# A retention block with a max-out feed-forward on one core: queries and keys of 28 chunks transposed by VectorE in 32x32 blocks instead of by TensorE

## The chip, the core and the metric

The kernel runs on one core of a Trainium2 chip. A core has five engines that run side by side and wait for each other through semaphores: TensorE (PE in the profile; its weight loads are shown apart as PEld), VectorE (DVE), ScalarE (ACT), GpSimd (POOL) and SyncE (SP), which here only issues DMAs. The metric is the device time of one execution in microseconds (us). Unchanged, the kernel takes 888.28 us (median of three runs, 887.31 to 889.44).

## The reference

Inputs are `q`, `k`, `v` of 8 batches x 8 heads x 576 positions x 64, float32, and four weight matrices in float64. Two parts follow each other:

```
# retention, per batch and head; gamma depends on the head
scores = (q @ k.T) / sqrt(64)
ret    = scores * (gamma ** (i - j) where i >= j, else 0)
x      = ret @ v                      # to [8 * 576, 8 * 64] = [4608, 512]
# feed-forward, w1, w2, w3: [512, 768], w_out: [768, 512]
h   = max(x @ w1, x @ w2, x @ w3)
out = h @ w_out                       # [4608, 512]
```

## The kernel before, in words

**Chunks.** The 8 x 576 = 4608 positions are cut into 36 chunks of 128 (`C`), `g` = 0 to 35. A chunk holds all 8 heads as 4 pairs (`NP`); a pair fills 128 partitions, 64 per head. For a chunk the kernel does, in this order:

- `load(g)`: one DMA each for k, q and v (two where a chunk crosses a batch), issued on SP; positions go on partitions, so a row of 8 heads x 64 numbers lands per partition.
- `decay_keys(g)`: GpSimd multiplies the keys by `gk`, gamma to the power minus the position (line 130).
- `transposes(g)`: TensorE transposes the decayed keys and the queries, four 128x128 pieces each, into PSUM (line 141); VectorE copies the keys (line 144), ScalarE the queries (line 146) to SBUF, as `kT` and `qT`.
- `scores(g)`: 8 matmuls of `kT` and `qT` (line 155), two masking products on VectorE (line 158), then 4 matmuls `kv` of keys and values (line 166) that bring the running state forward (lines 169 to 172).
- `values(g)`: 8 matmuls of the masked scores with v, and 4 of the old state with `qT` (lines 185, 190); VectorE multiplies by `gq`, gamma to the power plus the position, and the scale (line 192), into `xT`, the transposed input of the feed-forward.

**Groups.** Four chunks make a block of 512 tokens, `t` = 0 to 8, for the feed-forward `ffn(t)`. Block 0 multiplies plainly (`up_plain`), while the float64 weights are converted to float32 by VectorE, ScalarE and GpSimd (`conversion`). From block 1 on, `up` does each of 9 units (3 pairs of feature blocks x 3 weights) as seven half-size products (line 292), whose results VectorE and ScalarE combine: line 297 copies, lines 310, 320 and 323 add, lines 325, 331 and 332 take maxima. A unit needs line 320 to be done before its seventh product writes the same PSUM tile. Four `down` products (line 338) with a ScalarE copy and a DMA out on SP (lines 341, 342) end a block.

**Order.** The order is written out by hand. While block `t` runs, the chunks of block `t+1` are put between its units: `transposes`, one unit, `scores`, one unit, `values`, one unit, then the next chunk. So the block's first three chunks stand between the nine units, and the fourth chunk's steps before the first, second and third `down`. `load(g+1)` is called just before `transposes(g)`, and `decay_keys(g+1)` just before `scores(g)`. Each engine takes its own instructions strictly in this order; SP too, so a load that stands behind the DMAs out of a block is issued after them. DMAs on SP take eight semaphores in turn: each waits until the eighth DMA before it has landed. Raw tiles have four buffers each for k, q and v; a load also waits until its buffer has been read.

Of the kernel before, what the change touches and what calls it, by code (L numbers as in the profile page):

```python
# [26 lines left out]
FP32 = mybir.dt.float32  # L30
# [7 lines left out]
C = 128  # L38
NT = 4 * C
NH = NT // 2  # L40
AHEAD = 3
WAHEAD = 3

# [2 lines left out]
def kernel(  # L46
# [23 lines left out]
    CPT = NT // C  # L70
# [3 lines left out]
    wraw = ctx.enter_context(tc.tile_pool(name="wraw", bufs=WAHEAD))  # L74
    wtmp = ctx.enter_context(tc.tile_pool(name="wtmp", bufs=2))
    raw = ctx.enter_context(tc.tile_pool(name="raw", bufs=AHEAD + 1))
    kpool = ctx.enter_context(tc.tile_pool(name="kpool", bufs=3))
    att = ctx.enter_context(tc.tile_pool(name="att", bufs=2))
    stp = ctx.enter_context(tc.tile_pool(name="stp", bufs=2))
    xpool = ctx.enter_context(tc.tile_pool(name="xpool", bufs=2))  # L80
# [9 lines left out]
    gk = const.tile([C, H], FP32, name="gk")  # L90
# [14 lines left out]
    def start_of(g):  # L105
        r = -g * C % S
        return r if r < C else None

    masks = {0: causal, None: causal}
    for r in sorted({start_of(g) for g in range(NG)} - {0, None}):  # L110
        m = masks[r] = const.tile([C, C], FP32, name=f"causal{r}")
# [1 line left out]
        nc.gpsimd.memset(m[0:r, r:C], 0.0)  # L113


    raws, kds, qks, sts, states = {}, {}, {}, {}, {}

    def load(g):
        for n, src in (("k", k), ("q", q), ("v", v)):
            t = raws[n, g] = raw.tile([C, H, D], FP32, tag=n, name=n + "raw")  # L120
            row = 0
            while row < C:
                b, pos = divmod(g * C + row, S)
                n = min(C - row, S - pos)
                nc.sync.dma_start(t[row:row + n], src[b, :, pos:pos + n, :].rearrange("h p d -> p h d"))
                row += n

    def decay_keys(g):
        t = kds[g] = kpool.tile([C, H, D], FP32, tag="kd", name="kd")
        nc.gpsimd.tensor_tensor(t[:], raws.pop(("k", g))[:], gk[:].unsqueeze(2).to_broadcast([C, H, D]),  # L130
                                op=ALU.mult)

    def pair(t, p):
        return t[:, 2 * p:2 * p + 2, :].rearrange("a h d -> a (h d)")

    def transposes(g):
        both = {}
        for n, src in (("k", kds[g]), ("q", raws.pop(("q", g)))):
            pt = ps_r.tile([P, NP, C], FP32, tag="r", name=n + "t")
            for p in range(NP):  # L140
                nc.tensor.transpose(pt[:, p, :], pair(src, p), ident[:C, :C])  # L141
            t = both[n] = att.tile([P, NP, C], FP32, tag=n + "T", name=n + "T", bufs=2 if n == "k" else 3)
            if n == "k":
                nc.vector.tensor_copy(t[:], pt[:])
            else:
                nc.scalar.copy(t[:], pt[:])
        qks[g] = both

    def scores(g):
        qT, kT = qks[g]["q"], qks[g]["k"]  # L150
        s = [ps_r.tile([C, NP, C], FP32, tag="r", name=f"s{j}") for j in range(2)]
        for p in range(NP):
            for j in range(2):
                r = slice(D * j, D * (j + 1))
                nc.tensor.matmul(s[j][:, p, :], lhsT=kT[r, p, :], rhs=qT[r, p, :], start=True, stop=True)  # L155
        st = sts[g] = att.tile([C, 2, NP, C], FP32, tag="st", name="st", bufs=2)
        for j in range(2):
            nc.vector.tensor_tensor(st[:, j], s[j][:], masks[start_of(g)][:].unsqueeze(1).to_broadcast([C, NP, C]),  # L158
                                    op=ALU.mult)
        kd = kds.pop(g)  # L160
        if g + 1 == NG or start_of(g + 1) == 0:
            return
        r = start_of(g) or 0
        kv = ps_r.tile([P, NP, P], FP32, tag="r", name="kv")
        for p in range(NP):
            nc.tensor.matmul(kv[:, p, :], lhsT=pair(kd, p)[r:], rhs=pair(raws["v", g], p)[r:], start=True, stop=True)  # L166
        t = states[g + 1] = stp.tile([P, NP, P], FP32, tag="state", name="state")
        if start_of(g) is not None:
            nc.vector.tensor_tensor(t[:], kv[:], gs[:], op=ALU.mult)
        else:  # L170
            nc.vector.tensor_tensor(t[:], kv[:], states[g][:], op=ALU.add)  # L171
            nc.gpsimd.tensor_tensor(t[:], t[:], gs[:], op=ALU.mult)  # L172
# [3 lines left out]
    def values(g):  # L176
        old = C if start_of(g) is None else start_of(g)
        t, i = divmod(g, CPT)
        if i == 0:
            xT[t] = xpool.tile([P, NDC, NT], FP32, tag="xT", name="xT")  # L180
        st, vr, qT = sts.pop(g), raws.pop(("v", g)), qks.pop(g)["q"]
        o = ps_r.tile([P, NP, C], FP32, tag="r", name="o")
        for p in range(NP):
            for j in range(2):
                nc.tensor.matmul(o[D * j:D * (j + 1), p, :], lhsT=vr[:, 2 * p + j, :], rhs=st[:, j, p, :],  # L185
                                 start=(p == 0), stop=(old == 0 and p == NP - 1), skip_group_check=True)
        if old > 0:
            sd = states.pop(g)
            for p in range(NP):
                nc.tensor.matmul(o[:, p, :old], lhsT=sd[:, p, :], rhs=qT[:, p, :old],  # L190
                                 start=False, stop=(p == NP - 1), skip_group_check=True)
        nc.vector.tensor_tensor(xT[t][:, :, i * C:(i + 1) * C], o[:], gq[:], op=ALU.mult)  # L192
        if i == CPT - 1 and t > 0:
            x = xT[t]
            a11, a12, a21, a22 = (x[:, 2 * d:2 * d + 2, NH * r:NH * (r + 1)] for r in range(2) for d in range(2))
            s1, s2, s3, s4 = (spool.tile([P, 2, NH], FP32, tag=f"S{n}", name=f"S{n}") for n in (1, 2, 3, 4))
            nc.vector.tensor_tensor(s1[:], a21, a22, op=ALU.add)
            nc.vector.tensor_tensor(s2[:], s1[:], a11, op=ALU.subtract)
            nc.gpsimd.tensor_tensor(s3[:], a11, a21, op=ALU.subtract)
            nc.gpsimd.tensor_tensor(s4[:], a12, s2[:], op=ALU.subtract)  # L200
            xS[t] = {1: a11, 2: a12, 3: s4[:], 4: a22, 5: s1[:], 6: s2[:], 7: s3[:]}
# [77 lines left out]
    def convert(n):  # L279
        for _ in range(n):  # L280
            next(converting, None)

    def up(t, h, fp, i):

        f0, f1, lo, hi = 2 * fp, 2 * fp + 1, slice(0, NH), slice(NH, NT)
        x = ps_x.tile([P, NH], FP32, tag="x", name="x")
        y = {}
# [7 lines left out]
        def kept(name, src):  # L295
            c = ppool.tile([P, NH], FP32, tag=name, name=name)
            nc.scalar.copy(c[:], src[:])  # L297
            return c
# [77 lines left out]


    load(0)
    load(1)
    load(2)  # L380
    load_weights(1)
    load(3)
    load_weights(2)
    decay_keys(0)
    decay_keys(1)
    transposes(0)
    transposes(1)
    decay_keys(2)
    scores(0)
    transposes(2)  # L390
    values(0)
    decay_keys(3)
# [9 lines left out]
    decay_keys(4)  # L402
    convert(2)
    values(3)
    convert(4)
    for t in range(N // NT):
        work = ffn(t)
        for g in range((t + 1) * CPT, (t + 2) * CPT):
            for step in (transposes, scores, values):
                if g < NG:  # L410
                    if step is transposes and g + 1 < NG:
                        load(g + 1)
                    if step is scores and g + 1 < NG:
                        decay_keys(g + 1)
                    step(g)
                next(work, None)

# [50 lines left out]
```

## Time and profile before

| | |
|---|---|
| median of three runs | 888.28 us (887.31 to 889.44) |
| profiled execution, its own time | 889.22 us |
| its span, first to last instruction | 887.5 us |
| PE busy | 870.8 us, 98% of the span |
| DVE, ACT, POOL busy | 371.4, 185.8, 141.4 us |
| mean granted clock of TensorE | 0.996 |
| moved by the DMA queue of SP | 50.34 MB in 128064 packets |

Busy shares are means over stages with different limits, so the stretches of the span are looked at apart: a start of some 35 us in which the first chunks are loaded and computed, the block with the weight conversion up to about 145 us, seven blocks of 93 to 96 us each with four chunks in them, and a last block without chunks. An idle time in the profile carries the name of what ended it; idle time of an engine that nobody waits for costs nothing. Matmul durations overlap, so that the time a group of matmuls takes is read from the start of its first to the start of what follows.

### The profile page before, as it was taken

Reading aid. Unit: us, or ns where it says so; the run is one execution under the profiler, and the core shown is the slowest. Engines: PE = TensorE matmul, PEld = TensorE weight load, DVE = VectorE, ACT = ScalarE, POOL = GpSimd, SP = SyncE. Lnnn points to the kernel's source line nnn. Section 1 sums busy time; section 2 is a strip of 40 time slices with the busy share of each in tenths; the row PEclk is TensorE's granted clock in tenths of the full one; section 3 lists DMA queues with packets and bytes.
Section 4 is the critical chain, followed back from the end, with each engine's and each line's share of the span. In section 5 each row is a group of like instructions: output and inputs, shape, how many; then the busy total and the mean of one; then the engine's idle time right before and its main releaser. Section 6 shows DMA issues by size and latency. Waiting matters only on the chain.

```text
span 887.5 us, 11310 instructions
## 1 busy us (share of the span) xinstructions
PE 870.8 (98%) x4544; PEld 639.5 (72%) x4544; DVE 371.4 (42%) x681; ACT 185.8 (21%) x391; POOL 141.4 (16%) x128
## 2 busy tenths in 40 slices
PE   6999989999999999999999999999999999999998
PEld 5645546887588858885788668875888578866883
DVE  3899944553244423443244324432433334422330
ACT  2455521111111102111111111111111111111211
POOL 3444424221110111001210011101111111001000
PEclk9999989999999999999999999999999999999999
DMA  9545614200150006000600033001600050000001
GB/s 235 154 138 173 179 49 121 57 1 12 57 123 1 1 36 154 1 1 24 147 21 1 13 96 83 1 1 49 142 1 1 24 130 1 0 25 24 1 1 47
DMA packets 128547, 51.58 MB, mean 58 GB/s; under 512 B 113648, under 2 KB 122864, under 8 KB 128496
## 3 DMA queue, kind: packets, MB, share of 16 engines
q1 hardware_dynamic: 128064, 50.34, 21.5%
q8 instruction: 36, 0.59, 0.3%
q10 hardware_dynamic: 432, 0.53, 0.2%
q14 instruction: 15, 0.12, 0.0%
HBM read 41.42 MB, written 9.44 MB: 57 GB/s over the span
## 4 chain that ended last, share of the span: by engine, by line
PE 87%; DVE 5%; ACT 3%; issue 2%; POOL 1%; DMA 1%; SPq 0%; DVEq 0%; POOLq 0%; ACTq 0%
PE x L292 28%; PE down L338 21%; PE z L292 14%; PE y L292 7%; PE s L155 4%; PE o L185 3%; PE kv L166 3%; PE o L190 3%; PE kt L141 2%; PE qt L141 2%; ACT expo L244 1%; ACT expo L248 1%; DVE expo L241 1%; DVE expo L252 1%; DVE h L352 1%
## 5 line engine op out<-in xcount | busy, mean ns | idle before, releaser
L338 PE MATMUL down<-wout,h 128*128 128x512 f32 x432 | 191.7, 597 | 3.8 <-POOL wout L255 3.8
L338 PEld LDWEIGHTS down<-wout,h 128*128 128x128 f32 x432 | 80.5, 191 | 96.5 <-issue 90.7
L292 PE MATMUL x<-S,T 128*128 128x256 f32 x576 | 147.8, 379 | 0.0
L292 PEld LDWEIGHTS x<-S,T 128*128 128x128 f32 x576 | 109.2, 190 | 15.1
L172 POOL TENSOR_TENSOR state<-state,gs 128x512 f32<-128x512 f32 x24 | 31.5, 1311 | 343.5 <-DVE state L171 296.5
L158 DVE TENSOR_TENSOR st<-s,causal 128x512 f32<-128x512 f32 x72 | 46.4, 686 | 76.5 <-PE s L155 76.5
L292 PE MATMUL x<-xT,w 128*128 128x256 f32 x288 | 74.9, 382 | 0.0
L292 PE MATMUL x<-S,w 128*128 128x256 f32 x288 | 74.3, 380 | 0.0
L292 PE MATMUL z<-xT,T 128*128 128x256 f32 x288 | 73.9, 379 | 0.0
L292 PE MATMUL z<-S,w 128*128 128x256 f32 x288 | 73.9, 379 | 0.0
L292 PE MATMUL y<-xT,w 128*128 128x256 f32 x288 | 73.9, 379 | 0.0
L297 ACT COPY p<-x 128x256 f32<-128x256 f32 x72 | 26.8, 372 | 182.8 <-PE x L292 182.8
L320 DVE TENSOR_TENSOR tmp<-x,p 128x256 f32<-128x256 f32 x48 | 20.4, 425 | 104.4 <-PE x L292 104.4
L347 PE MATMUL up<-xT,w 128*128 128x512 f32 x144 | 63.4, 593 | 0.0
L341 ACT COPY osb<-down 128x512 f32<-128x512 f32 x36 | 21.1, 586 | 202.1 <-PE down L338 202.1
L292 PEld LDWEIGHTS z<-S,w 128*128 128x128 f32 x288 | 54.7, 190 | 7.4
L292 PEld LDWEIGHTS y<-xT,w 128*128 128x128 f32 x288 | 54.7, 190 | 7.4
L292 PEld LDWEIGHTS z<-xT,T 128*128 128x128 f32 x288 | 54.1, 189 | 8.1
L292 PEld LDWEIGHTS x<-S,w 128*128 128x128 f32 x288 | 49.4, 189 | 13.2 <-issue 1.1
L192 DVE TENSOR_TENSOR xT<-o,gq 128x512 f32<-128x512 f32 x36 | 24.8, 690 | 72.8 <-PE o L190 66.8
L292 PEld LDWEIGHTS x<-xT,w 128*128 128x128 f32 x288 | 49.8, 191 | 5.5 <-issue 0.8
L130 POOL TENSOR_TENSOR kd<-kraw,gk 128x512 f32<-128x512 f32 x36 | 38.3, 1068 | 85.5 <-DMA kraw<-in_k_dram 74.9
(61 smaller groups left out, 913.9 us busy)
## 6 DMA issues: line engine op xcount, KB each, us to landing
bits<-in_moe_w_dram SPq DMA_DIRECT2D x18, 512.0 KB, 3.6
out_dram<-osb SPq DMA_DIRECT2D x36, 256.0 KB, 2.0
kraw<-in_k_dram SPq DMA_DIRECT2D x32, 256.0 KB, 4.0
qraw<-in_q_dram SPq DMA_DIRECT2D x32, 256.0 KB, 4.3
vraw<-in_v_dram SPq DMA_DIRECT2D x32, 256.0 KB, 4.3
bits<-in_moe_w_out_dram SPq DMA_DIRECT2D x6, 512.0 KB, 3.4
kraw<-in_k_dram SPq DMA_DIRECT2D x8, 128.0 KB, 3.6
qraw<-in_q_dram SPq DMA_DIRECT2D x8, 128.0 KB, 3.2
```

The lines of the kernel that those rows point to most:

```text
L130: nc.gpsimd.tensor_tensor(t[:], raws.pop(("k", g))[:], gk[:].unsqueeze(2).to_broadcast([C, H, D]), op=ALU.mult)
L141: nc.tensor.transpose(pt[:, p, :], pair(src, p), ident[:C, :C])
L155: nc.tensor.matmul(s[j][:, p, :], lhsT=kT[r, p, :], rhs=qT[r, p, :], start=True, stop=True)
L158: nc.vector.tensor_tensor(st[:, j], s[j][:], masks[start_of(g)][:].unsqueeze(1).to_broadcast([C, NP, C]), op=ALU.mult)
L166: nc.tensor.matmul(kv[:, p, :], lhsT=pair(kd, p)[r:], rhs=pair(raws["v", g], p)[r:], start=True, stop=True)
L172: nc.gpsimd.tensor_tensor(t[:], t[:], gs[:], op=ALU.mult)
L185: nc.tensor.matmul(o[D * j:D * (j + 1), p, :], lhsT=vr[:, 2 * p + j, :], rhs=st[:, j, p, :], start=(p == 0), stop=(old == 0 and p == NP - ...
L190: nc.tensor.matmul(o[:, p, :old], lhsT=sd[:, p, :], rhs=qT[:, p, :old], start=False, stop=(p == NP - 1), skip_group_check=True)
L292: nc.tensor.matmul(out[:], lhsT=w[:, d * P:(d + 1) * P], rhs=xS[t][n][:, d, :], start=first and d == 0, stop=d == 1, skip_group_check=True)
L297: nc.scalar.copy(c[:], src[:])
L338: nc.tensor.matmul(ps[:], lhsT=h[:, fb, m * P:(m + 1) * P], rhs=w_sb["out", fb][:], start=(fb == 0), stop=(fb == NF - 1))
L347: nc.tensor.matmul(ps[:], lhsT=w_sb[i, fb][:, dc * P:(dc + 1) * P], rhs=xT[t][:, dc, :], start=(dc == 0), stop=(dc == NDC - 1))
```

## The change

Chunks 0 to 7 are transposed by TensorE as before (`BY_PE = 8`). For chunks 8 to 35:

- Queries are loaded in 32x32 blocks: 16 DMAs of 32 partitions x 4 pairs x 32 numbers (128 bytes in one piece, 16 KB each) per chunk. The keys are loaded so as well, in another 16 DMAs, into a tile `kx`. A block lands where it has to stand after its own transposition.
- VectorE transposes every 32x32 block in place of its row, one instruction of 128x512 for the keys and one for the queries, from SBUF to SBUF. There are no transposes on TensorE and no copies from PSUM for these chunks.
- The keys are also loaded as rows, as before, for the `kv` matmuls.

For all chunks the decay is taken off the keys and put on the values: GpSimd multiplies v by the same `gk` (`decay_values`), so the transposes read raw keys, and `kv` and the score-value products read decayed values. Buffers: q 4, `kx` 2, v 3, k rows 4. In chunks 4 to 7 the copy of the transposed keys moves from VectorE to ScalarE.

```
+BY_PE = 8
-    kpool = ctx.enter_context(tc.tile_pool(name="kpool", bufs=3))
+    vpool = ctx.enter_context(tc.tile_pool(name="vpool", bufs=3))
...
+    def spans(g):
+        row = 0
+        while row < C:
+            b, pos = divmod(g * C + row, S)
+            n = min(C - row, S - pos)
+            yield row, b, pos, n
+            row += n
 
     def load(g):
-        for n, src in (("k", k), ("q", q), ("v", v)):
-            t = raws[n, g] = raw.tile([C, H, D], FP32, tag=n, name=n + "raw")
...
+        rows = (("k", k), ("q", q), ("v", v)) if g < BY_PE else (("k", k), ("v", v))
+        for n, src in () if g < BY_PE else (("q", q), ("kx", k)):
+            t = raws[n, g] = raw.tile([P, NP, C // 32, 32], FP32, tag=n, name=n + "raw", bufs=4 if n == "q" else 2)
+            for blk in range(C // 32):
+                b, pos = divmod(g * C + 32 * blk, S)
+                for a in range(4):
+                    nc.sync.dma_start(
+                        t[32 * a:32 * a + 32, :, blk, :],
+                        src[b, a // 2::2, pos:pos + 32, 32 * (a % 2):32 * (a % 2) + 32].rearrange("p j i -> j p i"))
+        for n, src in rows:
+            t = raws[n, g] = raw.tile([C, H, D], FP32, tag=n, name=n + "raw", bufs=3 if n == "v" else 4)
+            for row, b, pos, m in spans(g):
+                nc.sync.dma_start(t[row:row + m], src[b, :, pos:pos + m, :].rearrange("h p d -> p h d"))
 
-    def decay_keys(g):
-        t = kds[g] = kpool.tile([C, H, D], FP32, tag="kd", name="kd")
-        nc.gpsimd.tensor_tensor(t[:], raws.pop(("k", g))[:], gk[:].unsqueeze(2).to_broadcast([C, H, D]),
+    def decay_values(g):
+        t = vds[g] = vpool.tile([C, H, D], FP32, tag="vd", name="vd")
+        nc.gpsimd.tensor_tensor(t[:], raws.pop(("v", g))[:], gk[:].unsqueeze(2).to_broadcast([C, H, D]),
                                 op=ALU.mult)
...
     def transposes(g):
-        both = {}
-        for n, src in (("k", kds[g]), ("q", raws.pop(("q", g)))):
+        both = qks[g] = {}
+        if g >= BY_PE:
+            for n in ("k", "q"):
+                t = both[n] = att.tile([P, NP, C], FP32, tag=n + "T", name=n + "T", bufs=2 if n == "k" else 3)
+                nc.vector.transpose(t[:].rearrange("a p c -> a (p c)"),
+                                    raws.pop(("kx" if n == "k" else n, g))[:].rearrange("a p b i -> a (p b i)"))
+            return
+        for n, src in (("k", raws["k", g]), ("q", raws.pop(("q", g)))):
...
-            if n == "k":
+            if n == "k" and g < CPT:
                 nc.vector.tensor_copy(t[:], pt[:])
             else:
                 nc.scalar.copy(t[:], pt[:])
...
-            nc.tensor.matmul(kv[:, p, :], lhsT=pair(kd, p)[r:], rhs=pair(raws["v", g], p)[r:], start=True, stop=True)
+            nc.tensor.matmul(kv[:, p, :], lhsT=pair(kr, p)[r:], rhs=pair(vds[g], p)[r:], start=True, stop=True)
...
-        st, vr, qT = sts.pop(g), raws.pop(("v", g)), qks.pop(g)["q"]
+        st, vr, qT = sts.pop(g), vds.pop(g), qks.pop(g)["q"]
...
-                        decay_keys(g + 1)
+                        decay_values(g + 1)
```

**TensorE, where a chunk's transposes stood.** The place is block 1, between the end of one unit (product `x<-S,w`, its seventh) and the begin of the next (`x<-xT,w`). Before:

```order
L292 MATMUL z<-xT,T_2_1_1303 128x256 x2
L292 MATMUL x<-S_1645,w_3_656 128x256 x2
L141 MATMUL kt<-ident,kd 128x128 x4
L141 MATMUL qt<-ident,qraw 128x128 x4
L292 MATMUL x<-xT,w_4_670 128x256 x2
L292 MATMUL y<-xT,w_4_670 128x256 x2
```

And with the change:

```order
L315 MATMUL z<-xT,T_2_1_1379 128x256 x2
L315 MATMUL x<-S_1765,w_3_656 128x256 x2
L315 MATMUL x<-xT,w_4_670 128x256 x2
L315 MATMUL y<-xT,w_4_670 128x256 x2
L315 MATMUL x<-S_1763,T_2_1_1378 128x256 x2
```

The eight transposes are gone, and the two units follow each other.

**VectorE, at the same kind of place.** It is the start of the unit that comes with the second chunk of block 1, behind the maxima of the unit before and, in this block alone, the weight sums `T`. Before:

```order
L332 TENSOR_TENSOR h<-h,tmp 128x512
L267 TENSOR_TENSOR T_1_1_1247<-w_3_596,w_2_576 128x256
L268 TENSOR_TENSOR T_1_1_1248<-w_3_596,T_1_1_1247 128x256
L144 COPY kT<-kt 128x512
L310 TENSOR_TENSOR h<-y,p_1277 128x256
L320 TENSOR_TENSOR h<-x,p_1290 128x256
```

And with the change:

```order
L355 TENSOR_TENSOR h<-h,tmp 128x512
L290 TENSOR_TENSOR T_1_1_1301<-w_3_596,w_2_576 128x256
L291 TENSOR_TENSOR T_1_1_1302<-w_3_596,T_1_1_1301 128x256
L159 STREAM_TRANSPOSE kT<-kxraw 128x512
L159 STREAM_TRANSPOSE qT<-qraw 128x512
L333 TENSOR_TENSOR h<-y,p_1353 128x256
L343 TENSOR_TENSOR h<-x,p_1366 128x256
```

The copy from PSUM has become two transposes from SBUF, which wait for DMAs and stand ahead of the unit's additions.

**SP, from the DMAs out of one block to the loads behind them.** Before:

```order
L342 DMA out_dram<-osb 128x512 x4
L125 DMA kraw<-in_k_dram 64x8x64 x2
L125 DMA qraw<-in_q_dram 64x8x64 x2
L125 DMA vraw<-in_v_dram 64x8x64 x2
L125 DMA kraw<-in_k_dram 128x8x64
L125 DMA qraw<-in_q_dram 128x8x64
L125 DMA vraw<-in_v_dram 128x8x64
```

And with the change:

```order
L365 DMA out_dram<-osb 128x512 x4
L138 DMA qraw<-in_q_dram 32x4x32 x16
L138 DMA kxraw<-in_k_dram 32x4x32 x16
L144 DMA kraw<-in_k_dram 64x8x64 x2
L144 DMA vraw<-in_v_dram 64x8x64 x2
L138 DMA qraw<-in_q_dram 32x4x32 x16
L138 DMA kxraw<-in_k_dram 32x4x32 x16
```

A chunk's loads have grown from 3 DMAs to 34 (36 where it crosses a batch), with the blocks of q and `kx` ahead of the rows of k and v.

More of the change, by code (lines that the diff above doesn't have):

```diff
@@ L113 @@
         nc.gpsimd.memset(m[0:r, r:C], 0.0)
-    raws, kds, qks, sts, states = {}, {}, {}, {}, {}
-    def load(g):
-        for n, src in (("k", k), ("q", q), ("v", v)):
-            t = raws[n, g] = raw.tile([C, H, D], FP32, tag=n, name=n + "raw")
[L121 to L126, printed above, removed]
-    def decay_keys(g):
-        t = kds[g] = kpool.tile([C, H, D], FP32, tag="kd", name="kd")
-        nc.gpsimd.tensor_tensor(t[:], raws.pop(("k", g))[:], gk[:].unsqueeze(2).to_broadcast([C, H, D]),
+    raws, vds, qks, sts, states = {}, {}, {}, {}, {}
+    def spans(g):
[5 more added lines that the diff above has]
+            row += n
+    def load(g):
+        rows = (("k", k), ("q", q), ("v", v)) if g < BY_PE else (("k", k), ("v", v))
[14 more added lines that the diff above has]
+        nc.gpsimd.tensor_tensor(t[:], raws.pop(("v", g))[:], gk[:].unsqueeze(2).to_broadcast([C, H, D]),
                                 op=ALU.mult)
@@ L146, in transposes @@
                 nc.scalar.copy(t[:], pt[:])
-        qks[g] = both
     def scores(g):
@@ L159, in scores @@
                                     op=ALU.mult)
-        kd = kds.pop(g)
+        kr = raws.pop(("k", g))
         if g + 1 == NG or start_of(g + 1) == 0:
@@ L383 @@
     load_weights(2)
-    decay_keys(0)
-    decay_keys(1)
+    decay_values(0)
+    decay_values(1)
     transposes(0)
     transposes(1)
-    decay_keys(2)
+    decay_values(2)
     scores(0)
@@ L391 @@
     values(0)
-    decay_keys(3)
+    decay_values(3)
     scores(1)
@@ L401 @@
     scores(3)
-    decay_keys(4)
+    decay_values(4)
     convert(2)
```

## The prediction

> **What bounds the kernel now.** I read the page's engine totals first, then the chain of waits by engine, then the stretches of the span.
>
> ```profile
> span 887.5 us, 11310 instructions
> PE 870.8 (98%) x4544; PEld 639.5 (72%) x4544; DVE 371.4 (42%) x681; ACT 185.8 (21%) x391; POOL 141.4 (16%) x128
> PE 87%; DVE 5%; ACT 3%; issue 2%; POOL 1%; DMA 1%; SPq 0%; DVEq 0%; POOLq 0%; ACTq 0%
> core 0: us, PE busy (x) PEld busy (x) DVE busy (x) ACT busy (x) POOL busy (x), PEclk, DMA share, GB/s
> 0.00:35.00 35.00, 25.77 (x223) 21.74 (x224) 19.80 (x33) 8.91 (x13) 13.53 (x20) 1.00 0.74 191
> 35.00:145.02 110.02, 106.18 (x414) 54.94 (x413) 85.94 (x125) 51.77 (x78) 44.57 (x36) 0.97 0.45 131
> 334.49:428.44 93.95, 93.95 (x509) 71.59 (x508) 34.13 (x66) 15.87 (x38) 9.99 (x8) 1.00 0.18 45
> ```
>
> The third stretch is one of the seven blocks that carry the 28 changed chunks: TensorE is busy in all 93.95 us of it, VectorE in 34, the DMA engines in 0.18. There a microsecond taken off TensorE is a microsecond off the end, as long as nothing else becomes late. In the first two stretches this does not hold: DVE has 86 of 110 us and the chain changes engines.
>
> **The time that the transposes take.** The timeline of PE shows it, at a chunk's begin within the units, before a `down`, and at a block's begin:
>
> ```profile
> 451.80 0.60 PE L141 MATMUL kt<-ident,kd 128*128 128x128 f32 x4
> 452.23 0.60 PE L141 MATMUL qt<-ident,qraw 128*128 128x128 f32 x4
> 452.67 0.60 PE L292 MATMUL x<-xT,w 128*128 128x256 f32 x2
> 402.67 0.60 PE L141 MATMUL kt<-ident,kd 128*128 128x128 f32 x4
> 403.54 1.45 PE L338 MATMUL down<-wout,h 128*128 128x512 f32 x3
> 428.44 0.60 PE L141 MATMUL kt<-ident,kd 128*128 128x128 f32 x4
> 429.31 1.03 PE L292 MATMUL x<-xT,w 128*128 128x256 f32 x4
> ```
>
> From the first transpose to the matmul behind them it is 0.87 us each time (452.67 - 451.80, 403.54 - 402.67, 429.31 - 428.44). **28 chunks x 0.87 = 24.4 us** come off PE. Chunk after chunk stands 451.80 - 428.44 = 23.36 us apart; without the transposes 22.5 us. That is the time in which everything below has to fit.
>
> **SP's issue.** A changed chunk has 34 DMAs instead of 3. The views of the tiles show what an issue costs:
>
> ```profile
> L342 SPq DMA_DIRECT2D out_dram<-osb x36: 332/332/360, 123.8 to 884.6; - x36
> DMA to landing us min/median/max: 2.0/2.0/4.0
> L125 SPq DMA_DIRECT2D kraw<-in_k_dram x40: 376/728/1794, 0.8 to 720.5; - x40
> DMA to landing us min/median/max: 2.7/4.0/5.8
> 429.30 0.33 SPq L342 DMA_DIRECT2D out_dram<-osb  x1
> 429.72 0.39 SPq L125 DMA_DIRECT2D kraw<-in_k_dram  x1
> 430.20 0.68 SPq L125 DMA_DIRECT2D qraw<-in_q_dram  x1
> 430.97 0.82 SPq L125 DMA_DIRECT2D vraw<-in_v_dram  x1
> q1 hardware_dynamic: 128064, 50.34, 21.5%
> ```
>
> Nearest to a 16 KB block (32 x 4 = 128 pieces of 128 bytes) is the DMA out, 128 rows of 2 KB: 0.33 us, next issue 0.42 us after it. The far end is a raw load, median 0.73 us, with the same 0.09 between about 0.82 from issue to issue. I take 0.42: the first load of a burst takes 0.39 though it has 1024 pieces, and only those behind it grow (0.68, 0.82), as they wait for pieces to be moved. The last row is a queue's packets, MB and share of 16 engines: a packet costs 0.215 x 16 x 887.5 / 128064 = 23.8 ns of one DMA engine, so 1024 pieces keep the 16 engines busy for 1.5 us, longer than an issue, but 128 pieces for 0.19 us, less than one. So 34 x 0.42 = 14.3 us of 22.5: hidden. The eight semaphores give 8 x 0.42 = 3.4 us for a landing, more than the 2.0 seen.
>
> The tight place is the second chunk of a block, whose loads stand behind the last DMA out. They start 1.28 us after the block's begin (429.72 - 428.44); the last of the 32 block loads lands at 1.28 + 32 x 0.42 + 2.0 = 16.7 us. VectorE comes to this chunk's transposes at 22.5 + 1.2 (the maxima ahead of them, below) = 23.7 us, so 7 us are left. The limit is (23.7 - 3.3) / 32 = 0.64 us an issue here, and 22.5 / 34 = 0.66 for the queue as a whole. The rows of k and v go out last and land at about 1.28 + 34 x 0.42 + 4.0 = 20 us. GpSimd's decay of v, now held by v and not by k, waits for that; behind it on GpSimd stands the state's product, wanted by `values` of the second chunk some 15 us later.
>
> **DMA engines.** Per chunk 1024 packets each for k and v, 2048 each for q and `kx`: 6144 x 23.8 ns / 16 = 9.1 us of 22.5, hidden, even though the keys are read twice. For 128-byte packets this price is rather too high, as the mean packet had 393 bytes.
>
> [...]
>
> **VectorE.** Two transposes of 128x512 from SBUF replace one copy from PSUM. No row shows such an operation. The rows that bound it:
>
> ```profile
> L144 DVE COPY kT<-kt x36: 677/684/693, 6.4 to 785.0; 128x512 f32<-128x512 f32 x36
> L246 DVE TENSOR_SCALAR frac<-bits x24: 414/1204/1522, 20.3 to 117.4; 128x512 int32<-128x512 int32 x24
> L198 DVE TENSOR_TENSOR S<-S,xT x8: 1636/1636/1637, 136.2 to 800.1; 128x512 f32<-128x512 f32 x8
> 396.52 1.13 PE L292 MATMUL x<-xT,w 128*128 128x256 f32 x4
> 401.21 0.43 DVE L320 TENSOR_TENSOR tmp<-x,p 128x256 f32<-128x256 f32 x1 [2.18 <-PE x L292]
> 403.20 0.68 DVE L332 TENSOR_TENSOR h<-h,tmp 128x512 f32<-128x512 f32 x1
> ```
>
> Between 0.41 and 1.64 us; I take 0.69, what most 128x512 operations take. The room: the unit before ends on PE at 402.67, its last maximum on DVE at 403.88, 1.2 us later. In a unit line 320 starts 4.7 us after the first product (401.21 - 396.52), when PE lets it. Line 310 (0.42) has to be done by then, so the transposes have from 1.2 to 4.3, 3.1 us, and need 1.4. Nothing is late. At 1.64 each they need 3.3: 0.2 us late, in the two chunks of a block that start between units (14 in all), and in block 1, with 1.05 us of weight sums there, twice more than 1 us: some 5 us in all. At a block's begin and before `down` DVE is free. [...]
>
> ScalarE loses 28 copies that nobody waited for. GpSimd's 36 products keep their size.
>
> **Start and block 0.** The transposes of chunks 0 to 7 stay, but no longer wait for GpSimd's product:
>
> ```profile
> 9.27 1.11 PE L141 MATMUL kt<-ident,kd 128*128 128x128 f32 x4 [1.79 <-POOL kd L130]
> 31.53 1.16 PE L190 MATMUL o<-qT,state 128*128 128x128 f32 x8
> 33.25 0.68 DVE L192 TENSOR_TENSOR xT<-o,gq 128x512 f32<-128x512 f32 x1
> 34.28 0.66 PE L141 MATMUL kt<-ident,kd 128*128 128x128 f32 x4 [1.59 <-POOL kd L130]
> 35.21 1.02 PE L347 MATMUL up<-xT,w 128*128 128x512 f32 x2
> ```
>
> At 9.27 GpSimd's 1.04 us fall away; the queries behind land a little after the keys, so I take 0.8. For chunk 4 the transposes can follow line 190 at 32.7, and the first `up` then waits for line 192, done at 33.9: 1.2 us before 35.21. Together 2.0 us. In chunks 4 to 7 a key copy moves from DVE (0.68) to ACT (0.59), both in the alternating chain of the conversion: taken as nothing; at best 4 x 0.68 = 2.7 us are won, at worst 4 x 0.59 = 2.3 lost and the 2.0 swallowed. The stretch has a granted clock of 0.97, 3.3 us lost (110 x 0.03), and that can come out otherwise by as much.
>
> **The sum**, against the profiled execution's own 889.2 us: 889.2 - 24.4 - 2.0 = 862.8. The median of the runs lies 0.9 below that execution, so **862 us**. Its own range: down to 862 - 2.7 - 3.3 = 856, up to 862 + 4.3 = 866, or 867 with the slow transposes.
>
> **Rivals.**
>
> *A. SP's issue becomes the bound (slower).* If a block load costs more than 0.66 us from issue to issue, SP cannot keep up in any block, each chunk's transposes come later than the one before, and behind them on VectorE stand lines 310 and 320, for which TensorE waits within a unit. For it: the raw loads' median of 0.82 with its gap. Against it: the 0.33 with 128 rows, and the 0.39 of an unhindered load. The gain is gone when a chunk takes 26.4 / 27 = 0.98 us more than 22.5, at 0.69 us an issue (27 chunks, since the first changed one is loaded early). At 0.82 a chunk takes 27.9 us, 5.4 x 27 = 146 us more: 1008 us. [...] Chance 0.06.
>
> *B. Part of the gain goes into waits of VectorE.* The block loads land late in the second chunk of each block only (0.64 to 0.66 us), or the transposes take well over 1.64 us. Three us in 7 blocks or 1 us in 14 chunks more than the 5 above: 862 + 5 to 862 + 21, so 867 to 883, with 872 the middle. For it: no row has the operation. Against it: 7 us and 1.7 us of room. Chance 0.09.
>
> *C. The transposes were filling.* Where they stood, TensorE may now stop for what ran behind them. For it: the first `down`, now 0.87 us earlier, reads with its fifth matmul the features of line 332; the first three of them take 1.45, so the fifth begins some 1.7 us behind 402.67, at 404.4, only 0.5 us after 403.88. Against it: this still fits, and elsewhere the unit behind reads nothing fresh. If it were lost in every fourth chunk: 7 x 0.87 = 6 us, 868. Chance 0.04.
>
> *D. The change doesn't bring the PE time off* (the units stretch, at some other bound): 888. The stretch in which PE is busy throughout speaks against it. Chance 0.02.
>
> **How the numbers follow.** The forecast has 0.79. The range: below 856 nothing is known to me; upward it takes in C and half of B: **856 to 872**, the likeliest's own being 856 to 867. A difference under 0.2% (1.8 us) could not be told from none. Faster by more: the forecast, B, C = 0.92; same: 0.02 (D); slower: 0.06 (A).
>
> **What would show it.** Right: some 22.5 us from chunk to chunk and blocks of about 90.5 us with PE busy in all of it; SP's block loads near 0.33 us each, a chunk's 34 within 15 us; the transposes near 0.69 us, with no wait of PE on lines 343 (320 before) or on `kT`. Wrong: idle time of DVE ended by a DMA of `kx` or q, growing from chunk to chunk (A) or in every fourth chunk alone (B); PE waiting on line 355 before `down` (C). If the blocks fit but the sum does not, it is the start: PE's first `up` should begin near 33 us, not 35.

## The result, and the profile after

With the change the kernel takes **861.04 us** (median of four runs, 859.42 to 861.36), against 888.38 us (887.31 to 889.44) without it: a ratio of 0.9687, 95% interval 0.9673 to 0.9702, or 27.3 us less. Forecast were 862, between 856 and 872. The profiled execution is the lowest of its four (859.42), so the two traces lie 29.8 us apart, 2.5 us more than the medians.

The totals of the page after, its chain of waits by engine, and the row of SP's queue (packets, MB, share of 16 engines):

```profile
span 857.7 us, 11778 instructions
PE 844.4 (98%) x4320; PEld 614.0 (72%) x4320; DVE 393.6 (46%) x705; ACT 171.4 (20%) x367; POOL 143.3 (17%) x128
PE 87%; DVE 6%; ACT 4%; issue 1%; DMA 1%; SPq 1%; POOL 0%; DVEq 0%; ACTq 0%
q1 hardware_dynamic: 227920, 57.74, 29.9%
```

PE lost 26.4 us of work and its share of the chain did not change. The queue moves 1.8 times the packets; SP's issues have 1% of the chain (0% before), DMA 1% as before. Three stretches of the span after are block 0 and blocks 1 and 3, which have changed chunks in them:

```profile
31.52:138.93 107.41, 104.41 (x408) 53.82 (x409) 86.95 (x124) 54.06 (x82) 45.97 (x37) 0.98 0.49 138
138.93:229.65 90.72, 90.67 (x478) 67.81 (x477) 44.01 (x84) 13.52 (x34) 21.39 (x22) 1.00 0.29 59
...
321.88:412.32 90.44, 90.44 (x477) 68.27 (x476) 37.11 (x70) 13.52 (x34) 9.67 (x8) 1.00 0.29 59
```

The columns are the stretch, its length, busy time of PE, PEld, DVE, ACT and POOL, granted clock, DMA share and GB/s. Block 3, 334.49 to 428.44 before with 93.95 us, is now 90.44 us long, and PE is still busy in all of it: the work that was taken off was not replaced by a wait. Set beside each other, by the start of the first feed-forward product of each block:

| part of the span | before, us | after, us | gained, us |
|---|---|---|---|
| start, up to the first `up_plain` | 35.2 | 31.5 | 3.7 |
| block 0, with the weight conversion | 110.5 | 107.4 | 3.1 |
| blocks 1 to 7 | 663.0 | 639.9 | 23.1 |
| block 8, without chunks | 78.8 | 78.9 | -0.1 |

How SP and VectorE carry their new work is seen at a chunk of block 1 on SP, at one of block 2 on VectorE, and in the views of the tiles:

```profile
157.80 8.02 SPq L138 DMA_DIRECT2D qraw<-in_q_dram  x16
165.92 7.49 SPq L138 DMA_DIRECT2D kxraw<-in_k_dram  x16
...
174.00 0.53 SPq L144 DMA_DIRECT2D vraw<-in_v_dram  x1
174.61 9.12 SPq L138 DMA_DIRECT2D qraw<-in_q_dram  x16
```

```profile
275.69 0.70 DVE L159 STREAM_TRANSPOSE kT<-kxraw 128x512 f32<-128x512 f32 x1
276.32 0.67 DVE L159 STREAM_TRANSPOSE qT<-qraw 128x512 f32<-128x512 f32 x1
...
279.14 0.42 DVE L343 TENSOR_TENSOR h<-x,p 128x256 f32<-128x256 f32 x1 [1.84 <-PE x L315]
279.73 1.03 PE L315 MATMUL x<-S,w 128*128 128x256 f32 x4
```

```profile
L138 SPq DMA_DIRECT2D kxraw<-in_k_dram x448: 312/430/1752, 112.9 to 739.1; - x150
DMA to landing us min/median/max: 1.6/1.8/3.5
L159 DVE STREAM_TRANSPOSE kT<-kxraw x28: 697/702/712, 135.3 to 755.9; 128x512 f32<-128x512 f32 x28
L159 DVE STREAM_TRANSPOSE qT<-qraw x28: 661/666/670, 135.9 to 756.5; 128x512 f32<-128x512 f32 x28
```

A chunk's 34 DMAs are issued from 157.80 to 174.61, in 16.8 us, 0.49 us each; a block load alone takes 0.43 in the median. The transposes take 0.70 and 0.67 us and start 0.63 us apart. Behind them line 343 still waits 1.84 us for PE: VectorE is early in that unit, not late.

Of PE's own waits after, these are the largest three, with the sum in us, how often, and the longest:

```profile
PE kt L165 <- DMA kraw<-in_k_dram: 4.6, 2, 4.1
PE down L361 <- POOL wout L278: 3.0, 2, 1.9
PE qt L165 <- DMA qraw<-in_q_dram: 1.4, 2, 1.2
```

They all belong to the first loads and to block 0. With the other rows of this view (0.4 and 0.2) PE waits 9.6 us in the whole execution, and never for a block load or a transpose of VectorE. This view, and the granted clock, decide most of the experiments below.

### The profile page after: what moved, and what is told of

Its sections match the earlier page's. It is cut to its first block, busy times and chain, and to the rows that moved or that the text cites. A ratio compares the mean times of both kernels' runs of the same rounds, so it can differ in the third digit from the quotient of the medians.

```text
span 857.7 us, 11778 instructions
## 1 busy us (share of the span) xinstructions
PE 844.4 (98%) x4320; PEld 614.0 (72%) x4320; DVE 393.6 (46%) x705; ACT 171.4 (20%) x367; POOL 143.3 (17%) x128
## 4 chain that ended last, share of the span: by engine, by line
PE 87%; DVE 6%; ACT 4%; issue 1%; DMA 1%; SPq 1%; POOL 0%; DVEq 0%; ACTq 0%
PE x L315 29%; PE down L361 21%; PE z L315 14%; PE y L315 7%; PE s L178 4%; PE o L208 4%; PE o L213 3%; PE kv L189 3%; ACT expo L267 2%; ACT expo L271 1%; DVE expo L275 1%; DVE expo L264 1%; DVE h L375 1%; DVE st L181 1%; DMA kraw<-in_k_dram 1%
## 5 line engine op out<-in xcount | busy, mean ns | idle before, releaser
L148 POOL TENSOR_TENSOR vd<-vraw,gk 128x512 f32<-128x512 f32 x36 | 38.7, 1076 | 499.5 <-DMA vraw<-in_v_dram 483.6
L343 DVE TENSOR_TENSOR tmp<-x,p 128x256 f32<-128x256 f32 x48 | 20.4, 425 | 104.4 <-PE x L315 104.4
L370 PEld LDWEIGHTS up<-xT,w 128*128 128x128 f32 x144 | 26.7, 190 | 30.9 <-issue 30.1
```

Of the source, the lines that this page charges most:

```text
L148: nc.gpsimd.tensor_tensor(t[:], raws.pop(("v", g))[:], gk[:].unsqueeze(2).to_broadcast([C, H, D]), op=ALU.mult)
L370: nc.tensor.matmul(ps[:], lhsT=w_sb[i, fb][:, dc * P:(dc + 1) * P], rhs=xT[t][:, dc, :], start=(dc == 0), stop=(dc == NDC - 1))
```

## The experiments

The theory is that of the prediction: 24.4 us come from eight transposes fewer on TensorE in each of 28 chunks, 2.0 us from transposes that no longer wait for GpSimd, and everything that takes their place is hidden, VectorE with 3.1 us of room in a unit and SP with 22.5 us for 34 issues. The rivals are that part of the gain has another source, and that what replaced the transposes stands close to its limit.

### Putting the transposes back: `undo_dve`, `pe_filler`

The first kernel lets TensorE do every chunk's transposes again, from raw keys and with the decay on the values; the second keeps VectorE's transposes and the block loads and only lets TensorE do eight transposes per changed chunk that nobody reads.

```
# undo_dve
-BY_PE = 8
+BY_PE = 36
# pe_filler, in transposes(g)
 if g >= BY_PE:
+    for n in ("k", "k"):
+        pt = ps_r.tile([P, NP, C], FP32, tag="r", name="idle")
+        for p in range(NP):
+            nc.tensor.transpose(pt[:, p, :], pair(raws[n, g], p), ident[:C, :C])
```

> All 36 chunks are transposed by TensorE again; the values stay decayed instead of the keys, and from chunk 4 on both copies from PSUM are ScalarE's. Theory (the transposes' own time on TensorE is the gain, 0.87 us in each of 28 chunks): 24.4 us come back, 861.0 + 24.4 = 885.4 us, blocks of 94 to 96 us again, while the first up product stays at 31.5 us, as in the changed kernel. Rival (most of the 27 us comes from the start and from the decay being off the path of the transposes): below 875 us.

> The changed kernel, with eight transposes per chunk from chunk 8 on put back on TensorE at their old place; they read the key rows, write PSUM and nobody reads them, so no copies out of PSUM. VectorE's transposes and all loads stay. Theory (TensorE's time alone counts): 28 x 0.87 = 24.4 us more, 885.4 us. Rival (the gain was the copies from PSUM and the PSUM buffers, with the waits on them): near 861, at most 868 us.

Measured: `undo_dve` 886.34 us (ratio to the kernel before 0.9974, 0.9963 to 0.9985), `pe_filler` 885.51 (0.9965, 0.9952 to 0.9977). In both the blocks are 93.9 and 95.7 us long again, with PE busy in all of it. Block 5 of `undo_dve` and block 3 of `pe_filler` (90.4 us each in the changed kernel):

```profile
522.28:616.23 93.95, 93.95 (x511) 71.58 (x510) 31.62 (x62) 17.71 (x43) 9.66 (x8) 1.00 0.18 46
```

```profile
330.28:424.23 93.95, 93.95 (x511) 71.58 (x510) 37.34 (x70) 13.50 (x34) 9.71 (x8) 1.00 0.28 57
```

So eight idle transposes a chunk take back 885.5 - 861.0 = 24.5 us, with the loads in 32x32 blocks and the transposes of VectorE in place and the copies from PSUM still gone; as the blocks with those copies (`undo_dve`) are no longer, the copies themselves were worth nothing. And what `undo_dve` keeps of the change is worth 888.4 - 886.3 = 2.1 us. That is the decay on the values, with the new buffer counts and with key copies on ScalarE, which no run takes apart; that the first `up_plain` comes at 32.97 us in it and at 35.21 before speaks for the decay. The theory holds in both terms.

### How much room VectorE has: `dve_twice`, `dve_thrice`, `dve_four`

Each transpose is done two, three or four times, the surplus ones into a spare tile ahead of the real one.

```
# dve_twice: 1, dve_thrice: 2, dve_four: 3 surplus ones
-nc.vector.transpose(t[...], raws.pop(...)[...])
+x = raws.pop(...)[...]
+for _ in range(1):
+    y = att.tile([P, NP, C], FP32, tag="spare", name="spare", bufs=1)
+    nc.vector.transpose(y[...], x)
+nc.vector.transpose(t[...], x)
```

> Each VectorE transpose is done twice, first into a spare tile. Theory (VectorE has 3.1 us at a unit's begin): four transposes at a pace of 0.63 us end 3.75 us after the unit's first product, the additions behind them just fit; only block 1 with its weight sums is late, by some 1 to 1.5 us in two chunks: 861 to 864 us. Rival (VectorE is already at the bound between the units): 14 chunks x 1.3 us = 18 us more, 879 us.

> Six transposes of VectorE per chunk instead of two (four: 863; eight: 931). At a pace of 0.63 us they end 1.2 + 6 x 0.63 = 5.0 us after the unit's first product; line 343 (0.42) with them ends at 5.8 or so, against the 5.2 at which TensorE wants its seventh product: 0.6 us late in 14 chunks of 27, 8 us, 869 us; with 1.2 us late 878. That holds if TensorE keeps its full clock. If stops of this size already halve the clock, as those of 2.4 us did with eight, 10 to 30 us more: 880 to 900.

> Each VectorE transpose is done four times, three times into a spare tile. Theory (3.1 us of room, then the product that waits for line 343 is late): eight transposes take 5.1 us, line 343 ends 7.0 us after the unit's first product instead of 5.0, against a limit of 5.2; 1.8 us late in each of 14 chunks and more in block 1: 861 + 26 + 3 = 890 us. Rival 1 (no room, all of it counts): 28 x 6 x 0.64 = 107 us more, 968 us. Rival 2 (VectorE is off the path altogether): 861 us.

Measured: 863.19 us (861.82 to 863.91) with four transposes a chunk, 880.09 (878.04 to 883.72) with six, 930.94 (923.99 to 935.30) with eight. The waits of PE for line 343, which stands three lines lower here, with six and with eight:

```profile
PE x L318 <- DVE h L346: 13.6, 14, 2.7
```

```profile
PE x L318 <- DVE h L346: 34.2, 14, 3.8
PE s L181 <- DVE qT L163: 10.4, 7, 1.8
```

Four fit, as the prediction's room of 3.1 us says (4 x 0.63 = 2.5), but for one stop of 1.0 us in block 1. Six need 3.8 us, and PE stops in 14 of the chunks, those that start between units, by 13.6 / 14 = 1.0 us on the mean; 0.6 to 1.2 had been expected, and with them 869 to 878 us. With eight the stops are 2.4 us (34.2 / 14), where the expectation had 1.8 and some 3 us more in block 1; the time is 41 us above it. PE also waits 10.4 us for the transposes themselves, and most of the rest is in the granted clock. Stretches of `dve_four` around one such stop, and its matmuls there:

```profile
403.00:405.00 2.00, 0.11 (x1) 0.00 (x0) 1.97 (x6) 0.00 (x0) 0.75 (x1) 1.00 0.55 103
405.00:407.00 2.00, 1.92 (x4) 1.13 (x4) 0.35 (x2) 0.00 (x0) 0.29 (x1) 0.54 0.22 33
407.00:409.00 2.00, 2.00 (x18) 1.85 (x18) 0.05 (x1) 0.37 (x1) 0.00 (x0) 0.61 0.22 34
```

```profile
402.09 1.03 PE L318 MATMUL z<-xT,T 128*128 128x256 f32 x4
405.08 2.03 PE L318 MATMUL x<-S,w 128*128 128x256 f32 x4 [1.96 <-DVE h L346]
```

PE stops for 1.96 us, and then works at half its clock for some 3.4 us: four matmuls of the same size take 2.03 instead of 1.03 us. The author's estimate of the time that this costs in an execution is its span times one minus its mean clock:

```profile
core 0: 933.6 us, clock 0.969
```

933.6 x 0.031 = 28.9 us. With the stops it gives the loss: see the balance further down. So the waits of this kernel cost about 1.6 times their length (75.9 us of span for 46.6 us of waits), and the expectation of 890 us had only their length.

### Two waits that should cost nothing: `rows_first`, `kt_dve`

The largest wait in the table after is this one (GpSimd's decay waiting for the values, which are issued behind 32 block loads):

```profile
POOL vd L148 <- DMA vraw<-in_v_dram: 483.6, 31, 29.0
```

`rows_first` issues the rows of k and v ahead of the block loads; `kt_dve` puts the key copy of chunks 4 to 7 back on VectorE.

```
# rows_first, in load(g)
+for n, src in rows:  ...          # moved here
 for n, src in () if g < BY_PE else (("q", q), ("kx", k)):  ...
-for n, src in rows:  ...
# kt_dve
-            if n == "k" and g < CPT:
+            if n == "k":
```

> Within a load the rows of k and v stand ahead of the blocks of q and keys. Theory (GpSimd's 484 us of waiting for v cost nothing but in block 1, where they delay the weight sums and stop TensorE for 0.2 to 0.3 us): most of that wait is gone, 860.5 to 861 us. Rival (the longest wait of the table costs time): some us less, 855 us. If the blocks become late in a block's second chunk, where they had 7 us, it would be slower.

> In chunks 4 to 7 the copy of the transposed keys is VectorE's again, not ScalarE's. Theory (both engines alternate in the conversion's chain, so that the move is worth nothing): 861 us, within 1 us. Rival (VectorE bounds block 0, 86 of 110 us busy): 4 x 0.69 = 2.7 us more, 863.7 us, with the first block's begin later than 138.9 us by that.

Measured: `rows_first` 860.91 us (860.63 to 861.17), `kt_dve` 862.61 (860.60 to 863.79). With the rows first the wait shrinks by 218 us,

```profile
POOL vd L148 <- DMA vraw<-in_v_dram: 265.6, 25, 16.6
```

and the kernel by 0.1 us, less than can be told apart. It is idle time of an engine with nothing due behind it, as the prediction had reckoned. `kt_dve` lies between what was expected of it and its rival, with overlapping runs; whether the move of those four copies brought anything stays open. In its trace block 0 is 2.3 us longer than in the changed kernel's, and 1.7 of them are half clock (6.8 us of it instead of 3.4).

### Where SP stops keeping up: `split_kx`, `split_all`, `split_kx_3`, `split_kx_out_act`

The block loads are cut in two (8 KB each), so that a chunk has more DMAs for the same bytes: 46 with 12 of the 16 key blocks cut, 50 with all of them, 66 with those of the queries too. In the fourth kernel there are 50, and ScalarE issues the DMAs out.

```
+parts = 2 if n == "kx" else 1        # split_kx; split_all: always 2; split_kx_3: n == "kx" and blk < 3
+for z in range(parts):
+    u = slice(z * NP // parts, (z + 1) * NP // parts)
     nc.sync.dma_start(
-        t[32 * a:32 * a + 32, :, blk, :], src[...].rearrange("p j i -> j p i"))
+        t[32 * a:32 * a + 32, u, blk, :], src[...][u].rearrange("p j i -> j p i"))
# split_kx_out_act: split_kx, and
-        nc.sync.dma_start(out[...], osb[:])
+        nc.scalar.dma_start(out[...], osb[:])
```

> Each of a chunk's 16 block loads of the keys is cut into two DMAs of half the pairs: 50 DMAs a chunk instead of 34, the same bytes and pieces. Theory (SP needs 0.474 us from issue to issue whatever the DMA holds; a block's second to fourth chunk are loaded one behind the other from 1.3 us after its begin): the fourth's blocks land at 3.3 + 2 x 23.7 + 22.8 = 73.5 us, 5 us behind the 68.4 at which VectorE comes to them, of which 1.7 are VectorE's room: 3.3 x 7 = 23 us more, 884 us. Rival (bytes or pieces set the loads' pace, not their number): 861 us. Rival (as the prediction priced it, 27 chunks x (23.7 - 22.5)): 893 us.

> The block loads of queries and keys are all cut into two: 66 DMAs a chunk, the same bytes and pieces. Theory (0.474 us an issue, three chunks in a row per block): the fourth chunk's blocks land at 3.3 + 2 x 31.3 + 30.3 = 96.2 us, 27.8 behind the need, less 1.7 of room: 26 x 7 = 182 us more, 1043 us. As the prediction priced it, 27 x (31.3 - 22.5): 1098 us. Rival (bytes or pieces set the pace): 861 us.

> Only three of four of the 16 key blocks are cut in two: 46 DMAs a chunk, 46 x 0.474 = 21.8 us on SP, less than the 22.5 us of a chunk, so that by the prediction's limit (0.66 us an issue with 34 DMAs, the same 22.5 us) nothing changes: 861. Theory after the first runs: a block needs 4 x 21.8 + some 6 us, since the DMAs out stand on SP between the loads and go only when the last down is done: 93.2 us instead of 91.4, so 861 + 7 x 1.9 = 874 (868 to 882), with TensorE waiting in the second chunk of a block or at the downs.

> As with the keys cut in two (50 DMAs a chunk), but the four DMAs out of a block are issued by ScalarE and no longer by SP. Theory: SP's loads alone take 4 x 50 x 0.485 = 97 us a block, and the further 6 to 8 us of the 105 us measured there come from the DMAs out, which stand on SP behind a chunk of loads and hold ScalarE's copies, TensorE's downs and in turn the next loads. Without them on SP the blocks are 97.5 us: 861 + 7 x 6.5 = some 906 us, instead of 960. If the half clock that was seen after stops of TensorE also goes, some us less. Rival: only the number of issues and the half clock matter, and the place of the DMAs out does not: 955 to 965.

Measured: `split_kx_3` 910.12 us (908.35 to 912.36), `split_kx` 960.11 (957.39 to 960.49), `split_all` 1163.87 (a single run; 1043 to 1098 expected), `split_kx_out_act` 936.90 (933.54 to 938.68). That bytes set SP's pace falls at once: half the bytes take the same time to issue, and it is their number that counts (the view of the tile in `split_kx`; the median of whole blocks was 430):

```profile
L141 SPq DMA_DIRECT2D kxraw<-in_k_dram x896: 311/425/1866, 114.7 to 854.5; - x180
```

The limit of the prediction agrees, if the whole chunk is counted: in `split_kx_3` a chunk's 46 DMAs take some 23.2 us on SP (from 437.72 to 460.92), 0.50 each, just over the 22.5 that a chunk has. But all four cost far more than was expected. A surplus of 0.7 us a chunk is 19 us in 27 chunks, and 49 were measured; in `split_kx`, 50 x 0.49 = 24.5, so 2.0 x 27 = 54 (with 0.474 it would be 32), and 99 were measured. Two things explain it. One is the place of the DMAs out. They stand on SP behind a chunk of loads of the block after, and in front of the next chunk's; where SP is behind, ScalarE waits for them with its copies, and PE waits for ScalarE. PE's waits in `split_kx`, and below them VectorE's and ScalarE's:

```profile
PE y L318 <- ACT osb L367: 31.7, 6, 7.4
PE x L318 <- DVE h L346: 15.7, 7, 3.5
```

```profile
DVE kT L162 <- DMA kxraw<-in_k_dram: 115.7, 23, 12.7
ACT osb L367 <- DMA out_dram<-osb: 102.9, 6, 18.5
```

A stretch of it, at a block's end (two rows of SP, then one of ScalarE):

```profile
348.76 0.39 SPq L147 DMA_DIRECT2D kraw<-in_k_dram  x1
349.86 5.58 SPq L368 DMA_DIRECT2D out_dram<-osb  x4
353.87 1.21 ACT L367 COPY osb<-down 128x512 f32<-128x512 f32 x2 [18.28 <-DMA out_dram<-osb]
```

The four DMAs out could go only when the loads were issued. They then hold SP for 5.6 us, so that the next chunk's loads begin later still: the `down` products are done by 347.4, but ScalarE has two tiles for its copies, and the last two copies wait until the first two DMAs out have landed. `split_kx_out_act` takes them off SP, and 23 of the 99 us go. It was expected to bring 54, because it was thought that nothing else stood behind the loads. What now does is an input difference for the feed-forward (`S<-xT`, line 225): it stands on GpSimd behind the decay of the values, and that waits for the row of v, the last of 50 DMAs. PE's wait, and GpSimd's timeline:

```profile
PE z L318 <- POOL S L225: 43.8, 6, 9.3
```

```profile
446.82 1.04 POOL L151 TENSOR_TENSOR vd<-vraw,gk 128x512 f32<-128x512 f32 x1 [26.45 <-DMA vraw<-in_v_dram]
...
449.04 1.26 POOL L225 TENSOR_TENSOR S<-xT 128x512 f32<-128x512 f32 x1
```

That is the very wait that `rows_first` had shown to cost nothing: so it is with 34 DMAs a chunk, but with 50 it holds PE at the begin of six blocks. The other thing is the clock again: in and after such stops the granted clock was 0.50, here up to 10 us at a time.

### The same for chunks 4 to 7: `by_pe_4`

```
-BY_PE = 8
+BY_PE = 4
```

> Chunks 4 to 7 transposed by VectorE too, from 32x32 blocks. They stand in block 0, where TensorE is not what ends the block but the chain of the weights' conversion, with VectorE busy for 86 of 110 us. Theory: 4 x 0.87 us off TensorE bring nothing there, VectorE gets 4 x 1.3 us more in the chain, and 4 x 32 more issues on SP come between the loads of the weights: 866 to 885 us. Rival: the gain of the other chunks goes on, 861 - 4 x 0.87 = 857.5 us, and this would be the better kernel.

Measured: 901.63 us (900.89 to 902.96; ratio to the kernel before 1.0156, 1.0141 to 1.0171). The gain of the other 28 chunks is all there, their blocks are 90.4 and 92.4 us long; but block 0 takes 148.4 us instead of 107.4. SP at its begin and in its first part, where two loads of weights (line 253) now stand behind 36 DMAs of a chunk, and in the changed kernel behind six:

```profile
29.95 9.16 SPq L138 DMA_DIRECT2D kxraw<-in_k_dram  x16
...
42.07 1.12 SPq L253 DMA_DIRECT2D bits<-in_moe_w_dram  x2
43.24 9.35 SPq L138 DMA_DIRECT2D qraw<-in_q_dram  x16
...
61.07 0.53 SPq L144 DMA_DIRECT2D vraw<-in_v_dram  x1
```

These two go at 42.07; in the changed kernel they went at 30.89. Each chunk adds its 17 to 18 us on SP, and the last of the 24 weight loads goes at 145.7 instead of 104.4, 41 us later: as much as was lost. The conversion waits for weights, and PE for the conversion. Of the three reasons in the expectation only the one on SP is of that size (VectorE's 4 x 1.3 us make 5 at most), and its price was not in the range given. With this the step of the change at chunk 8 is seen to matter: the first block loads come behind the last weights, at 104.80.

### The balance of stops and clock

For each of these kernels, in us: how much longer its profiled span is than the changed kernel's 857.7, the sum of PE's waits beyond the 9.6 above, and the span times one minus the mean clock, beyond the 1.7 of the changed kernel (857.7 x 0.002).

| kernel | span | waits of PE | half clock | the two together |
|---|---|---|---|---|
| `dve_thrice` | 20.4 | 14.4 | 2.7 | 17.1 |
| `dve_four` | 75.9 | 46.6 | 27.2 | 73.8 |
| `split_kx_3` | 50.5 | 28.9 | 20.1 | 49.0 |
| `split_kx_out_act` | 74.1 | 53.6 | 27.2 | 80.8 |
| `split_kx` | 98.0 | 67.8 | 34.6 | 102.4 |
| `by_pe_4` | 42.3 | 33.2 | 20.8 | 54.0 |

Where PE stops while its clock is halved, the last column counts that time one and a half times. PE waits so for 19.0 us in `by_pe_4`, 21.6 in `split_kx_out_act`, 17.1 in `split_kx` and 6.9 in `split_kx_3`; without half of that their sums are 44.5, 70.0, 93.9 and 45.6. So the two views account for the loss to within some 5 us in all six kernels. No kernel that was tried is faster than the changed one by more than its runs scatter.

## Why the prediction was right, point by point

**What bounds the kernel.** Right, and shown: in blocks 1 to 7 PE is busy throughout before and after, and idle work on it costs its full time (`pe_filler`: 24.5 us for 28 x 0.87 = 24.4).

**28 x 0.87 = 24.4 us.** Right in mechanism and size. Measured 24.5 with the transposes put back on PE, 25.3 with all of VectorE's part undone. In the two traces blocks 1 to 7 give 23.1 and chunk 8, in block 0, another 0.87: 24.0. The missing 0.3 us is mostly in block 1, where PE's seventh product of a unit came 0.2 us late behind VectorE: GpSimd's weight sums, held up by its wait for v, ran beside VectorE's, which took 0.8 to 0.9 instead of 0.42 us each:

```profile
160.63 1.04 POOL L148 TENSOR_TENSOR vd<-vraw,gk 128x512 f32<-128x512 f32 x1 [13.84 <-DMA vraw<-in_v_dram]
162.15 0.94 DVE L290 TENSOR_TENSOR T<-w,w 128x256 f32<-128x256 f32 x1
163.12 0.83 DVE L291 TENSOR_TENSOR T<-w,T 128x256 f32<-128x256 f32 x1
165.41 0.40 DVE L343 TENSOR_TENSOR h<-x,p 128x256 f32<-128x256 f32 x1
165.86 1.13 PE L315 MATMUL x<-S,w 128*128 128x256 f32 x4
```

With the rows of v loaded first, this block took 90.40 instead of 90.72 us, so the 0.3 comes from the late v.

**Start, 2.0 us.** 2.1 in the runs (`undo_dve`). The two traces differ by 3.7 up to the first `up_plain`, and that row should have stood near 33 by the prediction:

```profile
31.52 7.13 PE L370 MATMUL up<-xT,w 128*128 128x512 f32 x16 [0.42 <-DVE xT L215]
```

In the profiles of the other kernels it stands between 32.3 and 33.7 us, so 1 to 2 us of the 3.7 are this execution's own. Block 0 came out 3.1 us shorter, 0.87 by chunk 8's transposes, 1.7 by half the time at half clock (3.4 us from 117.3 instead of 6.8 from 120.8); the prediction had named that clock as something that can come out otherwise, in its range and not in its sum. With 24.5 and 2.1 the two terms make 26.6 of the 27.3 us; no run assigns the remaining 0.7.

**SP's issue, 0.42 us.** A size that was off: 0.47 within a burst in the median and 0.49 with the rows of k and v, so 16.8 us a chunk instead of 14.3. It was hidden, as 22.5 were at hand. The landings, 1.8 us each in the median, overlap: 34 DMAs take 16.8 us.

**DMA engines.** The 9.1 us a chunk were too high, as the prediction had said of them: a share of 0.29 in a block of 90.4 us is 6.6 us a chunk, the DMAs out included.

**VectorE.** 0.70 and 0.67 us against 0.69, and a room of 3.1 us in a unit: the first is right, and the second lies between the 2.5 us of four transposes, which fit (863.2), and the 3.8 of six, which do not (880.1).

**The far ends.** Two prices were wrong, and both too low, because a wait had been priced by its length. Rival A, SP as the bound, priced as the prediction does it, was to cost 1.2 us x 27 = 32 us at 50 DMAs, and costs 99: when SP is behind, DMAs out and the values come late too, and the balance has 34.6 us of half clock beside 67.8 us of waits. Rival B priced late transposes at their lateness in 14 chunks; with eight transposes a chunk the lateness of 2.4 us comes to 34 us, 10 more are waits for the transposes themselves, and 27 are half clock. Neither was needed for the forecast, but the chance and the range rested on them: the cost of being wrong was two to three times what was reckoned (99 for 32 us with A, 70 for 29 with eight transposes).

**C and D.** Neither came about: PE waits for no `down` behind line 355, and each of the seven blocks is shorter by what was taken out of it, to within 0.3 us.

## What to carry to other kernels

Work that was moved off the bounding engine was worth its pitch in the timeline there, times its count (28 x 0.87 = 24.4 us, and 24.5 measured), as long as each engine that took it over had room at the very place; both can be read ahead from one trace, and the room is better read from the unit's timeline than from busy shares. SP's queue was used up by the number of DMAs (0.425 us each at 8 KB, 0.430 at 16 KB), and what stood behind the loads in it came late: results going out (ScalarE waited 18.3 us in `split_kx`), weights (41 us later in `by_pe_4`), a tensor that another engine decays (GpSimd waited 26.5 us in `split_kx_out_act`). So before adding DMAs, list what stands behind them. And price a wait of TensorE of some 2 us or more at more than its length, as half clock followed 12 of the 14 stops of 2.0 to 3.8 us in `dve_four`.

## What the runs showed of the hardware that was not expected

Some short stops of PE were followed by half its granted clock. In `dve_four`, in blocks 1 to 7, 12 of the 14 stops of 2.0 to 3.8 us were followed by 3.4 or 6.8 us at half clock, and none of the seven of 1.4 to 1.8 us; in `dve_thrice` the one of 2.7 us was, and none of the 13 of up to 1.4; once, in `split_kx_3`, a stop of 1.4 us was as well. The stretches at half clock are all 3.4 us or a multiple of it, up to 17.1 in `by_pe_4`, and within one execution their begins all lie a multiple of 3.41 us apart. Why they have this length, no run shows.

What followed a stop went with where it lay between these begins, as the trace of `dve_four` shows when it is divided into pieces of 3.41 us at them. In blocks 1 to 7, half clock followed each of the 12 pieces at full clock in which PE was idle for 1.96 us or more, and none with 1.66 or less. A stop of 1.96 us that lies in one piece (PE busy 1.45 us) is followed by a clock of 0.50; one of 2.83 us that is shared by two (PE busy 2.00 and 2.01 us) is not:

```profile
504.15:507.56 3.41, 1.45 (x8) 0.80 (x8) 2.47 (x6) 0.01 (x1) 0.00 (x0) 1.00 0.67 148
507.56:510.97 3.41, 3.41 (x24) 3.30 (x24) 1.29 (x2) 0.36 (x1) 1.04 (x1) 0.50 0.33 53
...
678.23:681.64 3.41, 2.00 (x10) 1.42 (x8) 3.31 (x6) 0.37 (x1) 0.00 (x0) 1.00 0.23 34
681.64:685.06 3.42, 2.01 (x20) 1.62 (x20) 1.69 (x5) 0.37 (x1) 0.00 (x0) 1.00 0.24 36
```

The other stop that half clock did not follow, of 2.71 us, is shared as well. In the other kernels the two kinds are not apart: pieces with 1.40 us (`split_kx_3`) and 1.62 us (`split_kx_out_act`) idle were followed, and one with 2.00 us (`split_all`) was not. Why some stretches last 6.8 us though PE is busy all through the first half, as behind 507.56, stays open.

DMAs of 8 KB (`split_kx`) and of 16 KB (the changed kernel) took SP the same time, 0.425 and 0.430 us in the median: between these two sizes the price on the queue went by the DMA, not by the byte.
